# A range-test branch taken ahead of the last outputs, one output on another queue, and fewer closing waits

## The chip, the cores and the metric

The kernel runs on one core of one Trainium2 chip. The metric is the device time of one execution in microseconds (us), and of several executions the median. A profiled execution also has a *span*, from the first to the last instruction of the program; in most kernels here the time is 1.7 to 2.2 us longer than the span. The **tail** is the end of the span minus the end of the last matmul.

## The reference, cut to what matters

```python
# x: 2048 x 1024, 32 heads of 32
g = sigmoid((x * gate_w).sum(-1, keepdims=True))
a = linear_attention(x, A_wqkv) @ A_wo       # phi(t) = where(t > 0, t + 1, exp(t)) + 1e-6
b = local_attention(x, B_wqkv) @ B_wo        # 8 keys, every second position back; softmax
return g * a + (1 - g) * b
```

The kernel's fast path leaves out the subtraction of the row maximum in the softmax and folds some products. This is allowed only while the values lie in a certain range. It therefore computes maxima on the way, turns them into one flag, and at the end branches: if the flag is 0, a second complete program (the general path) computes everything again. With the given inputs the flag is 1, and the general path is jumped over.

## The kernel before

A small scheduler in Python places all operations of the fast path in time and emits them engine by engine; then each engine runs `tail`:

```python
def run(e, eng):                       # in Prog.emit
    for o, waits in plan[eng]:
        for s, v in waits:
            e.wait_ge(s, v)
        ins = o.fn(e)
        ins.then_inc(o.val[0], 16 if o.chan is not None else 1)
    tail(e, eng)

def tail(e, eng):
    reg = e.alloc_register("fast_ok")
    e.wait_ge(*flag_op.val)            # VectorE has written the flag
    e.reg_load(reg, flag[0:1, 0:1])
    if eng == "sp":
        for s, v in P.final:           # every DMA channel of the program: 80
            e.wait_ge(s, v)
    with e.If_eq(reg, 0):
        for s, v in P.final + [...]:   # (cut)
            e.wait_ge(s, v)
        for th in progs[eng]:          # the general path of this engine
            th(e)
```

The last stage computes 16 output tiles of 128 x 1024. For each half tile TensorE does 8 matmuls, VectorE combines the result with the other branch into the buffer `o` (two buffers in turn), and SyncE sends a whole tile to memory. The last tile goes in three pieces of 512, 256 and 256 columns:

```python
parts = [(0, 512), (512, 1024)] if t < NT - 1 else [(0, 512), (512, 768), (768, 1024)]
for f0, f1 in parts:
    # 8 matmuls into a bank of PSUM, then on VectorE the combine (cut)
    if t == NT - 1 or f1 == 1024:
        c = f0 if t == NT - 1 else 0
        P.op("sp", lambda e, ...: e.dma_start(out2[...], o_[:, c:f1]), 0.5, ..., chan="out%d_%d" % (os_, c))
```

Of the kernel before, what the change touches and what calls it, by code (L numbers as in the profile page):

```python
# [18 lines left out]
PADK = 16  # L19
PADV = 14  # L20
SCALE = DH ** -0.5
SZ = {BF16: 2, F32: 4, I32: 4}


class Tile:


    def __init__(self, space, h, lo, shape, dtype):
# [3 lines left out]
        for n in shape[1:]:  # L32
            self.row *= n
        self.size = SZ[dtype]

# [3 lines left out]
    def all(self):  # L39
        return [(self.space, self.lo, self.lo + self.row * self.size, self)]  # L40
# [21 lines left out]
class Prog:  # L62
# [136 lines left out]
                    ready(u, ready_at[u])  # L199
        self.span = max(free.values())  # L200

    def emit(self, block, tail):
        for e in self.ENGS:
            self.esem[e] = self.sem("e_" + e)
        chan_n = {}
        order = sorted(self.ops, key=lambda o: (o.start, o.seq))
        known_at = {}
        known = {e: {} for e in self.ENGS}
        plan = {e: [] for e in self.ENGS}
        cnt = {e: 0 for e in self.ENGS}  # L210
        for o in order:
            if o.chan is not None:
                if o.chan not in self.csem:
                    self.csem[o.chan] = self.sem("c_" + o.chan)
                chan_n[o.chan] = chan_n.get(o.chan, 0) + 16
                o.val = (self.csem[o.chan], chan_n[o.chan])
            else:
                cnt[o.eng] += 1
                o.val = (self.esem[o.eng], cnt[o.eng])
            need = {}  # L220
            k = known[o.eng]
            deps = sorted(o.deps, key=lambda d: -d.start)
            for d in deps:
                if d.eng == o.eng and d.chan is None:
                    if o.eng == "pe":
                        continue
                s, v = d.val
                if k.get(s.num, 0) >= v:
                    continue
                need[s.num] = (s, max(v, need.get(s.num, (s, 0))[1]))  # L230
                k[s.num] = max(k.get(s.num, 0), v)
                for s2, v2 in known_at[d].items():
                    if k.get(s2, 0) < v2:
                        k[s2] = v2
            known_at[o] = dict(k)
            plan[o.eng].append((o, list(need.values())))

        def run(e, eng):
            for o, waits in plan[eng]:
                for s, v in waits:  # L240
                    e.wait_ge(s, v)
                ins = o.fn(e)
                ins.then_inc(o.val[0], 16 if o.chan is not None else 1)
            tail(e, eng)

        self.final = [(self.csem[c], n) for c, n in chan_n.items()]
        self.counts = cnt
        block.sync(lambda e: run(e, "sp"))
        block.scalar(lambda e: run(e, "act"))
        block.tensor(lambda e: run(e, "pe"))  # L250
        block.vector(lambda e: run(e, "dve"))
        block.gpsimd(lambda e: run(e, "pool"))
# [63 lines left out]
def general_path(nc, A_x, A_wqkv, A_wo, B_wqkv, B_wo, gate_w, out):  # L316
# [254 lines left out]
    with ExitStack() as esA2:  # L571
# [40 lines left out]
        for jj, (kind, j) in enumerate(chunks):  # L612
# [13 lines left out]
            for u in range(NU):  # L626
# [28 lines left out]
                elif kind == "qB":  # L655
                    cA_q = pb.op("act", lambda e, j=j, ps_set=ps_set, scol=scol: e.activation(qT_sb[:, j, scol], ps_set, ACT.Copy, scale=SCALE),
                                 waits=[(sT, cT)], inc=sA)
# [445 lines left out]
def build_kernel(nc, A_x, A_wqkv, A_wo, B_x, B_wqkv, B_wo, gate_w, out):  # L1103
# [5 lines left out]
    out2 = out[0].rearrange("(m e) d -> e m d", e=2)  # L1109
# [4 lines left out]
    def SB(shape, dtype, name, at=None):  # L1114
        n = SZ[dtype]
        for d in shape[1:]:
            n *= d
        if at is None:
            at = base[0]
            base[0] += (n + 31) // 32 * 32  # L1120
        uid[0] += 1
        h = nc.alloc_sbuf_tensor_at("%s_%d" % (name, uid[0]), list(shape), dtype, offset=at)
        return Tile("S", h, at, list(shape), dtype)
# [94 lines left out]
    act = lambda n: 0.19 + n / 1200.0  # L1218
    dps = lambda n: 0.14 + n / 960.0

    def plan(seen):

        P = Prog(nc, nc.alloc_semaphore)
# [85 lines left out]
        def group(bank, lhs, rhs, reads, lo=0, hi=8):  # L1309
            def fn(e):  # L1310
                last = None
                for dc in range(lo, hi):
                    last = e.matmul(bank.ap(), lhs(dc), rhs(dc), start=(dc == 0), stop=(dc == 7))  # L1313
                return last
            return P.op("pe", fn, (hi - lo) * mm(512), reads=reads, writes=[bank.iv])
# [25 lines left out]
        def move(dst, src, n, bank, reg, scale=None, reads=()):  # L1341

            if scale is None:
                fd = lambda e: e.tensor_copy(dst, src())  # L1344
                fa = lambda e: e.activation(dst, src(), ACT.Copy)  # L1345
            else:
                fd = lambda e: e.tensor_scalar(dst, src(), scale, None, op0=ALU.mult)
                fa = lambda e: e.activation(dst, src(), ACT.Copy, scale=scale)  # L1348
            P.op("any", {"act": fa, "dve": fd}, {"act": act(n) + (0.1 if reads else 0.0), "dve": dps(n)}, reads=[bank.iv] + list(reads), writes=[reg])
# [7 lines left out]
        for t, half in [(4 * b + i, half) for b in range(NT // 4) for half in range(2) for i in range(4)]:  # L1357
# [5 lines left out]
            for d in range(0, 8, step):  # L1363
                o = group(bank, xs, w, [xr, ws[0].part((d, d + step), (half * 512, half * 512 + 512))], d, d + step)
# [87 lines left out]
        def slot(rate):  # L1452
            slot_n[0] += 1
            while later and later[0][0] <= slot_n[0]:
                later.pop(0)[1]()
            while states and states[0][0] <= slot_n[0]:
                states.pop(0)[1]()
            pace[0] = min(pace[0] + rate, 1.0) if todo else 0.0
            if todo and pace[0] >= 1.0:
                pace[0] -= 1.0  # L1460
                fill(*todo.pop(0))
# [6 lines left out]
        for e_ in range(2):  # L1468
            if True:
                for j in range(8):  # L1470
                    for isq in range(2):
                        for u in (2 * e_, 2 * e_ + 1):
# [6 lines left out]
                            reg = tgt.part((j, j + 1), (u * 512, (u + 1) * 512))  # L1479
                            move(dst, bank.ap, 512, bank, reg, SCALE if isq else None)  # L1480
                            slot(FILL)
# [63 lines left out]
        for c in range(4):  # L1545
            for r in range(4):
                k = 4 * (c % 2) + r
# [75 lines left out]
        def final(t):  # L1623
            tgt, c0 = a_loc(t)
            o_, os_ = osb.next()
            e_, r = t // 8, t % 8
            parts = [(0, 512), (512, 1024)] if t < NT - 1 else [(0, 512), (512, 768), (768, 1024)]
            for f0, f1 in parts:
                bank = main.next()
                n = f1 - f0  # L1630

                def fn(e, t=t, bank=bank, f0=f0, f1=f1):
                    for dc in range(8):
                        last = e.matmul(bank.ap(0, f1 - f0), qT[:, dc, t * 128:(t + 1) * 128], ws[3][:, dc, f0:f1], start=(dc == 0), stop=(dc == 7))  # L1634
                    return last
                P.op("pe", fn, 8 * mm(n), reads=[qT.part((0, 8), (t * 128, (t + 1) * 128)), ws[3].part((0, 8), (f0, f1))], writes=[bank.iv])
                i0, i1 = f0 // 128, f1 // 128
                P.op("dve", lambda e, bank=bank, o_=o_, t=t, n=n, i0=i0, i1=i1, tgt=tgt, c0=c0: e.scalar_tensor_tensor(  # L1638
                    out=o_[:, i0 * 128:i1 * 128].rearrange("p (i s) -> p i s", s=128), in0=bank.ap(0, n).rearrange("p (i s) -> p i s", s=128),
                    scalar=gm[:, t:t + 1], in1=tgt[:, i0:i1, c0:c0 + 128], op0=ALU.mult, op1=ALU.add), dps(n),  # L1640
                    reads=[bank.iv, gm.all(), tgt.part((i0, i1), (c0, c0 + 128))], writes=[o_.part((f0, f1))])
                if t == NT - 1 or f1 == 1024:
                    c = f0 if t == NT - 1 else 0
                    P.op("sp", lambda e, e_=e_, r=r, o_=o_, c=c, f1=f1: e.dma_start(out2[e_, r * 128:(r + 1) * 128, c:f1], o_[:, c:f1]), 0.5,
                         reads=[o_.part((c, f1))], chan="out%d_%d" % (os_, c), lat=1.0)

        nums = [(u, j) for u in range(4) for j in range(8)]
# [37 lines left out]
        flag_op = P.op("dve", lambda e: e.tensor_tensor(flag[:, :], mx1[:, 0:1], mx1[:, 2:3], ALU.mult), 0.1, reads=small, writes=[flag.all()], prio=1e5)  # L1685


        for t in range(EARLY, NT):
            final(t)
# [13 lines left out]
    P, flag_op = best[:2]  # L1703
    ps_guard.__exit__(None, None, None)
    progs, es_g = general_path(nc, A_x, A_wqkv, A_wo, B_wqkv, B_wo, gate_w, out)

    def tail(e, eng):
        reg = e.alloc_register("fast_ok")
        e.wait_ge(*flag_op.val)
        e.reg_load(reg, flag[0:1, 0:1])  # L1710
        if eng == "sp":
            for s, v in P.final:
                e.wait_ge(s, v)
        with e.If_eq(reg, 0):
            for s, v in P.final + [(P.esem[x], n) for x, n in P.counts.items() if n]:
                e.wait_ge(s, v)
            for th in progs[eng]:
                th(e)

    with nc.Block() as block:  # L1720
        P.emit(block, tail)
    es_g.__exit__(None, None, None)
    return P

# [31 lines left out]
```

## Time and profile before

| | before |
|---|---|
| time, median of 3 | 495.43 us (495.07 to 496.56) |
| span of the profiled execution | 493.6 us |
| TensorE busy | 477.7 us, 97% |
| end of the last matmul | 488.03 us |
| end of the last combine on VectorE | 488.55 us |
| tail | 5.61 us |

The page of the profiled execution shows what bounds the kernel (busy time, share, instructions, then the waits' chain by engine):

```profile
PE 477.7 (97%) x5055; PEld 226.2 (46%) x5121; DVE 274.7 (56%) x487; ACT 166.9 (34%) x287; POOL 5.1 (1%) x27
...
PE 89%; DMA 3%; SPq 3%; issue 2%; DVE 2%; ACT 1%; ACTq 0%
```

TensorE works nearly without a gap until 488. The timeline of the end (start, duration, engine, line, what) shows that nothing counted as work comes after 488.55, 5 us before the end:

```profile
485.37 4.03 SPq L1644 DMA_DIRECT2D out_dram<-o  x4
486.32 1.36 DVE L1638 SCALAR_TENSOR_TENSOR o<-ps_all,gm,xT 128x512 bf16<-128x512 f32 x2 [0.98 <-PE ps_all L1634]
488.07 0.48 DVE L1638 SCALAR_TENSOR_TENSOR o<-ps_all,gm,xT 128x256 bf16<-128x256 f32 x1 [0.39 <-PE ps_all L1634]
```

What happens in those 5 us is done by the engines' sequencers, and is seen when one asks for the lines of `tail` themselves. The columns are: how many, shortest/median/longest duration in ns, first and last start in us. Line 1710 is the load of the flag, 1713 the list of waits, 1714 the branch, 1720 the close of the program. The profile writes an engine's sequencer with a final q.

```profile
L1710 SPq TENSOR_LOAD <-flag x1: 503/503/503, 489.5 to 489.5; - x1
```

```profile
L1713 SPq EVENT_SEMAPHORE  x40: 28/28/28, 490.0 to 492.8; - x40
```

```profile
L1714 ACTq COMPARE_BRANCH  x1: 50/50/50, 443.7 to 443.7; - x1
L1714 PEldq COMPARE_BRANCH  x1: 3644/3644/3644, 486.3 to 486.3; - x1
L1714 DVEq COMPARE_BRANCH  x1: 72/72/72, 488.7 to 488.7; - x1
L1714 SPq COMPARE_BRANCH  x1: 58/58/58, 492.9 to 492.9; - x1
```

```profile
L1720 ACTq DRAIN  x1: 66/66/66, 446.1 to 446.1; - x1
L1720 PEldq DRAIN  x1: 73/73/73, 490.0 to 490.0; - x1
L1720 DVEq DRAIN  x1: 58/58/58, 491.5 to 491.5; - x1
L1720 SPq DRAIN  x1: 57/57/57, 493.4 to 493.4; - x1
```

Read the branch and the drain of an engine together. VectorE branches at 488.7 and does its next instruction at 491.5: the branch record says 72 ns, but the engine stood for 2.9 us. TensorE's sequencer stood for 3.6 us (its matmuls ran on meanwhile, until 488.03), ScalarE (443.7 to 446.1) for 2.4. In each of these stalls the trace shows a packet of instructions arrive: 8 KB from 489.70 to 490.16 in VectorE's, 8 KB from 444.57 to 445.00 in ScalarE's, 16 KB from 487.45 to 488.55 in TensorE's. I call such an arrival a fetch, and what one packet brings a block. (The packets come in two queues: 42 of 16 KB in one and, inside the span, 8 KB each in the other. I put the 16 KB queue down to TensorE and the other to the remaining engines, by the stalls that their packets fall into.) SyncE is the exception: 0.5 us from branch to drain.

### The profile page before, as it was taken

The page shows a single profiled execution, that of the slowest core. Times are in us where ns is not written, and L with a number is a line of the kernel's source. Part 1 is how long each engine was busy: PE and PEld are TensorE (multiplying, and loading weights), DVE is VectorE, ACT ScalarE, POOL GpSimd, SP SyncE. Part 2 cuts the span into 40 slices and gives each one's busy share as a digit, 9 for nine tenths or more (in the row PEclk, how much of TensorE's full clock was granted, in tenths as well). Part 3 has the DMA queues.
Part 4 walks back from the last instruction along what each step waited for, and adds up shares of the span by engine and source line. Part 5 has one row for each costly group of instructions (what it writes and reads, how often), then busy time and mean ns, then how long its engine had stood idle before and what let it go on. Part 6 is the DMA issues. An engine that isn't in the chain of part 4 may idle for free.

```text
span 493.6 us, 11394 instructions
## 1 busy us (share of the span) xinstructions
PE 477.7 (97%) x5055; PEld 226.2 (46%) x5121; DVE 274.7 (56%) x487; ACT 166.9 (34%) x287; POOL 5.1 (1%) x27
## 2 busy tenths in 40 slices
PE   8999999999999999999999999999999999999995
PEld 3444444444444445545554544444444444444442
DVE  2112345899676785564555555596865735524443
ACT  2111111222334345656565465455432223020000
POOL 3000000000000000000000000000000000000000
PEclk9999999999999999999999999999999999999999
DMA  8989992222003155111010100503564325101122
GB/s 225 212 206 322 307 371 62 86 86 85 14 23 110 29 161 141 28 36 35 24 35 25 35 3 3 171 1 80 124 182 117 76 38 153 65 1 66 65 85 68
DMA packets 51067, 48.80 MB, mean 99 GB/s; under 512 B 20161, under 2 KB 38977, under 8 KB 51010
## 3 DMA queue, kind: packets, MB, share of 16 engines
q1 hardware_dynamic: 50466, 47.47, 34.5%
q8 instruction: 42, 0.69, 0.6%
q10 hardware_dynamic: 544, 0.52, 0.3%
q14 instruction: 15, 0.12, 0.1%
HBM read 34.34 MB, written 9.44 MB: 89 GB/s over the span
## 4 chain that ended last, share of the span: by engine, by line
PE 89%; DMA 3%; SPq 3%; issue 2%; DVE 2%; ACT 1%; ACTq 0%
PE ps_all L1313 71%; PE ps_all L1634 11%; PE ps_all L1405 2%; PE ps_all L1424 2%; DMA rb<-rc_hbm 1%; SPq L1287 1%; PE ps_all L1506 1%; SPq L1598 1%; DMA w<-in_B_wqkv_dram 1%; PE ps_all L1431 1%; DMA rc_hbm<-ra 1%; DVE zsel L1548 1%; SPq L1292 1%; DVE pq L1326 0%; PE ps_all L1585 0%
## 5 line engine op out<-in xcount | busy, mean ns | idle before, releaser
L1313 PE MATMUL ps_all<-w,xT 128*128 128x512 bf16 x921 | 207.5, 380 | 5.4 <-issue 4.3
L1313 PE MATMUL ps_all<-xT,w 128*128 128x512 bf16 x748 | 167.5, 379 | 2.3 <-issue 1.7
L1313 PEld LDWEIGHTS ps_all<-w,xT 128*128 128x128 bf16 x960 | 91.3, 98 | 109.8 <-DMA xT<-in_A_x_dram 1.8
L1313 PEld LDWEIGHTS ps_all<-xT,w 128*128 128x128 bf16 x768 | 73.7, 98 | 89.1 <-issue 1.8
L1634 PE MATMUL ps_all<-w,qT 128*128 128x512 bf16 (+1 forms) x259 | 55.3, 373 | 0.3
L1634 PEld LDWEIGHTS ps_all<-w,qT 128*128 128x128 bf16 x264 | 25.8, 98 | 29.7
L1324 DVE TENSOR_SCALAR e<-e 128x512 bf16<-128x512 bf16 x64 | 18.3, 291 | 33.8 <-ACT e L1320 17.2
L1344 DVE CAST vst<-ps_all 128x512 bf16<-128x512 f32 x15 | 10.4, 692 | 44.0 <-PE ps_all L1313 44.0
L1411 ACT ACTIVATE E<-ps_all 128x1824 bf16<-128x1824 f32 (+1 forms) x18 | 30.4, 1687 | 9.8 <-PE ps_all L1405 9.0
L1322 ACT ACTIVATE e<-ps_all 128x512 bf16<-128x512 f32 x32 | 19.1, 597 | 42.8 <-PE ps_all L1313 42.8
L1414 DVE TENSOR_TENSOR E<-E,msk 128x1824 bf16<-128x1824 bf16 (+1 forms) x18 | 19.8, 1102 | 22.1 <-ACT E L1411 22.1
L1638 DVE SCALAR_TENSOR_TENSOR o<-ps_all,gm,xT 128x512 bf16<-128x512 f32 (+1 forms) x25 | 18.2, 730 | 23.0 <-PE ps_all L1634 22.8
L1320 ACT ACTIVATE e<-ps_all 128x512 bf16<-128x512 f32 x32 | 19.1, 597 | 26.8 <-PE ps_all L1313 25.8
L1345 ACT ACTIVATE vst<-ps_all 128x512 bf16<-128x512 f32 x17 | 10.1, 597 | 47.7 <-PE ps_all L1313 47.7
L1274 DVE TENSOR_TENSOR mx<-mx,kT 128x1024 bf16<-128x1024 bf16 x32 | 20.8, 688 | 9.3 <-ACT kT L1345 9.2
L1274 DVE TENSOR_TENSOR mx<-mx,qT 128x1024 bf16<-128x1024 bf16 x32 | 20.8, 687 | 6.9 <-ACT qT L1348 6.7
L1443 DVE TENSOR_TENSOR qT<-ps_all,L 128x456 bf16<-128x456 f32 (+1 forms) x36 | 21.0, 627 | 6.2 <-ACT L L1441 5.0
L1326 DVE SCALAR_TENSOR_TENSOR pk<-ps_all,e 128x512 bf16<-128x512 f32 x32 | 21.9, 688 | 0.7
L1440 ACT ACTIVATE L<-ps_all 128x456 f32<-128x456 f32 (+1 forms) x36 | 17.8, 547 | 12.4 <-PE ps_all L1424 12.4
L1345 ACT ACTIVATE kT<-ps_all 128x512 bf16<-128x512 f32 x16 | 9.6, 597 | 35.8 <-PE ps_all L1313 35.8
L1601 DVE TENSOR_TENSOR xT<-xT,rb 128x512 bf16<-128x512 bf16 x24 | 16.3, 689 | 8.7 <-DMA rb<-rc_hbm 8.5
L1348 ACT ACTIVATE qT<-ps_all 128x512 bf16<-128x512 f32 x16 | 9.6, 597 | 31.5 <-PE ps_all L1313 31.5
(72 smaller groups left out, 284.1 us busy)
## 6 DMA issues: line engine op xcount, KB each, us to landing
rb<-rc_hbm SPq DMA_DIRECT2D x32, 256.0 KB, 5.1
w<-in_A_wqkv_dram SPq DMA_DIRECT2D x6, 1024.0 KB, 8.5
v<-vB_hbm SPq DMA_DIRECT2D x36, 128.0 KB, 2.9
vB_hbm<-vst SPq DMA_DIRECT2D x32, 128.0 KB, 5.9
w<-in_B_wqkv_dram SPq DMA_DIRECT2D x4, 1024.0 KB, 9.0
xn<-in_A_x_dram SPq DMA_DIRECT2D x16, 256.0 KB, 2.7
out_dram<-o SPq DMA_DIRECT2D x15, 256.0 KB, 2.0
w<-in_A_wo_dram SPq DMA_DIRECT2D x8, 256.0 KB, 4.1
```

What stands on the lines that cost most here:

```text
L1274: P.op("dve", lambda e, m=m, op=op: e.tensor_tensor(m[:, 0:n], m[:, 0:n], src, op), 0.08 + n / 1920.0, reads=[m.all(), reg], writes=[m.all()],
L1313: last = e.matmul(bank.ap(), lhs(dc), rhs(dc), start=(dc == 0), stop=(dc == 7))
L1320: P.op("act", lambda e: e.activation(e_[:, :], bank.ap(), ACT.Exp), act(512), reads=[bank.iv], writes=[e_.all()])
L1322: P.op("act", lambda e: e.activation(e_[:, :], bank.ap(), ACT.Exp, accum_out=qe[:, col:col + 1]), act(512) + 0.1, reads=[bank.iv], writes= ...
L1324: P.op("dve", lambda e: e.tensor_scalar(e_[:, :], e_[:, :], 1.0, 1e-6, op0=ALU.min, op1=ALU.add), 0.25, reads=[e_.all()], writes=[e_.all()])
L1326: P.op("dve", lambda e: e.scalar_tensor_tensor(out=dst, in0=bank.ap(), scalar=0.0, in1=e_[:, :], op0=ALU.max, op1=ALU.add), dps(512), read ...
L1345: fa = lambda e: e.activation(dst, src(), ACT.Copy)
L1411: P.op("act", lambda e: e.activation(E[:, 0:32 * nq].rearrange("p (j q) -> p j q", j=4), ps[:, 4:8, 0:8 * nq], ACT.Exp), act(32 * nq), rea ...
L1414: P.op("dve", lambda e: e.tensor_tensor(ev(), ev(), m[:, :, :].rearrange("p r q -> p (r q)")[:, None, :].to_broadcast([128, 16, 2 * nq]), ...
L1443: P.op("dve", lambda e, L=L, h=h, q0=q0: e.tensor_tensor(qT[:, :, q0:q0 + nq], SO[h].ap(0, n).rearrange("p (c q) -> p c q", c=8), L[:, 0:n ...
L1634: last = e.matmul(bank.ap(0, f1 - f0), qT[:, dc, t * 128:(t + 1) * 128], ws[3][:, dc, f0:f1], start=(dc == 0), stop=(dc == 7))
L1638: P.op("dve", lambda e, bank=bank, o_=o_, t=t, n=n, i0=i0, i1=i1, tgt=tgt, c0=c0: e.scalar_tensor_tensor(out=o_[:, i0 * 128:i1 * 128].rear ...
```

## The change

The intent has three parts. (1) SyncE, VectorE and ScalarE take the branch *before* their last operations, and the remaining operations stand in both arms; the branch's stall then falls into time in which these engines have slack (19, 14 and 30 us ahead of the scheduled end; TensorE keeps its branch last). (2) The very last output piece is issued by ScalarE, not SyncE. (3) In the taken arm SyncE waits only for the four channels whose last transfer nobody has waited for.

```diff
+BACK = {"sp": 19, "dve": 14, "act": 30}
@@ emit
         def run(e, eng):
-            for o, waits in plan[eng]:
-                ...
-            tail(e, eng)
+            ops = plan[eng]
+            k = len(ops)
+            while k and ops[k - 1][0].start > max(self.span - BACK.get(eng, 0), flag_op.end + 3):
+                k -= 1
+            go(e, ops[:k])
+            tail(e, eng, lambda: go(e, ops[k:]))
+        self.last = [(self.csem[c], n) for c, n in chan_n.items() if not self.awaited(c)]
@@ final(t)
-                    P.op("sp", lambda e, ...
+                    P.op("act" if f1 == 1024 and c else "sp", lambda e, ...
@@ tail
-        if eng == "sp":
-            for s, v in P.final:
-                e.wait_ge(s, v)
         with e.If_eq(reg, 0):
+            rest()
             ...                        # (cut) waits and general path
+        with e.Else():
+            rest()
+            if eng == "sp":
+                for s, v in P.last:
+                    e.wait_ge(s, v)
```

## The prediction

> **What bounds the kernel.** TensorE. The page's busy table has PE at 477.7 of 493.6 us (97%), the granted clock at 0.998, and the chain of waits is 89% PE. The change touches none of this: no matmul, eviction or load goes away. It can only change what follows the last matmul.
>
> **The tail now** (timeline and raw instruction records of the last 8 us). The last matmul ends at 488.04, the last VectorE combine runs 488.07 to 488.55. SyncE issues the output in three last pieces: at 487.10 (0.33 us), 487.71 (1.22 us, unusually long) and 488.97 (0.43 us). So the last issue waits 0.42 us for the queue, not for its data. Then SyncE loads the flag (489.46, 0.50 us), executes 40 double semaphore waits from 490.00 to 492.82 (about 61 ns each after the first few, one pause of 0.4), branches at 492.86, drains at 493.36; the closing barrier ends at 493.64. The last output piece has landed by 490.68 (15 of 16 signals) or 491.05 (the last). So the wait list, not the transfer, ends last: about 1.8 us of it runs with nothing outstanding. The other engines' taken branches cost a fetch: GpSimd 2.5 us, ScalarE 2.4, VectorE 488.66 to 491.54 (2.9), TensorE 486.26 to 489.90 (3.6). [...] SyncE's own branch took only 0.5 us.
>
> **What the change does.**
> 1. Only four output channels remain to be waited for, instead of 80 semaphores: removes nearly all of the 2.8 us wait list. What then ends last is the landing.
> 2. Flag load, and branch of SyncE, move about 19 us ahead: takes 0.55 us between last issue and first wait and the 0.45 us closing jump off the end.
> 3. The last piece goes through ScalarE's idle queue: issue near 488.6 instead of 488.97; saves 0.3 to 0.4 us of landing. The middle piece on SyncE (landed 490.04 to 490.28) then ends about as late.
> 4. VectorE's load and fetch (0.54 + 2.9 us) move to about 475. This stalls VectorE in the output stage, where it has 0.75 us of work per 1.73 us of TensorE: the next combine is about 2.5 us late, and 0.98 us is recovered per combine, so it is level by 482. Spare PSUM banks keep TensorE going. SyncE's fetch falls after the issue at 468.1, with 3.4 us to the next: at most one output a little late. TensorE's branch stays where it is, ending at 489.96, just ahead of the new end.
>
> New end, estimated: last landing 490.3 to 490.6, last waits 0.1, drain 0.06, barrier 0.28: 490.7 to 491.1. So 2.5 to 2.9 us come off the span, all on the critical path (0.5%); the rest of the changed work was hidden before and stays hidden.
>
> **Prediction: 492.7 us, range 491.9 to 493.5 (8 in 10). Faster by over 2%: 0.01; within 2%: 0.98; slower by over 2%: 0.01.**
>
> **What would show it.** Span near 490.9; last combine still ending near 488.55; no SyncE list of waits after the last issue; the end within 0.6 us of the last landing; PE gapless through 470 to 488; VectorE with one hole of about 3.5 us near 475 and shorter gaps after it until about 482; last issue on ScalarE's queue near 488.6.
>
> **What would make it wrong.** The hole in VectorE or SyncE reaching TensorE through PSUM or the two output buffers (then over 494); another fetch stall at the end of the taken arm (up to 3 us given back); TensorE's fetch getting longer and setting the end; the last piece's issue on ScalarE being as slow as SyncE's 1.22 us, or its landing held by a fetch; another operation order chosen by the scheduler.

## The result and the profile after

| | before | after |
|---|---|---|
| time, median of 6 | 495.5 us (495.07 to 496.56) | 492.72 us (491.94 to 494.49) |
| ratio | 1 | 0.9949 (0.9927 to 0.997) |
| span of the profiled execution | 493.6 us | 492.6 us |
| end of the last matmul in it | 488.03 us | 489.52 us |
| tail | 5.61 us | 3.10 us |

Ratios in this document are the mean time of one kernel's fast runs over the mean of the other's fast runs of the same rounds, so they are not quite the ratio of the medians.

The profiled execution of after happens to be its slowest (494.49 us; the spans of the other five are 490.1 to 492.4). Its first matmul after the warm-up began at 6.47 us instead of 5.62, and its last ended 1.5 us later than in the profile of before. Of these 1.5 us, 0.85 are the start; the rest arises on the way, and the other five spans show that it is not typical. It is why the two profiled spans differ by only 1.0 us while the tails differ by 2.5.

The lines of `tail` after (1724 is the branch, 1734 the waits, 1736 the close):

```profile
L1724 ACTq COMPARE_BRANCH  x1: 50/50/50, 445.1 to 445.1; - x1
L1724 SPq COMPARE_BRANCH  x1: 57/57/57, 470.5 to 470.5; - x1
L1724 DVEq COMPARE_BRANCH  x1: 72/72/72, 476.3 to 476.3; - x1
L1724 PEldq COMPARE_BRANCH  x1: 3704/3704/3704, 487.8 to 487.8; - x1
```

```profile
L1734 SPq EVENT_SEMAPHORE  x2: 17/22/28, 492.1 to 492.1; - x2
```

```profile
L1736 DVEq DRAIN  x1: 524/524/524, 489.6 to 489.6; - x1
L1736 ACTq DRAIN  x1: 152/152/152, 490.5 to 490.5; - x1
L1736 PEldq DRAIN  x1: 73/73/73, 491.5 to 491.5; - x1
L1736 SPq DRAIN  x1: 13/13/13, 492.4 to 492.4; - x1
```

SyncE now ends when the last output has landed, 2.54 us after the last matmul. All branches over the general path but TensorE's are over long before. (SyncE has one more branch, at the end of its arm: its record says 43 ns, and the next instruction begins 0.17 us after it.) So the sum was forecast well. But two things in the profile do not fit the forecast. The first is VectorE's hole, in the timeline of VectorE:

```profile
475.73 0.75 DVE L1651 SCALAR_TENSOR_TENSOR o<-ps_all,gm,xT 128x512 bf16<-128x512 f32 x1 [0.97 <-PE ps_all L1647]
482.20 2.73 DVE L1651 SCALAR_TENSOR_TENSOR o<-ps_all,gm,xT 128x512 bf16<-128x512 f32 x4 [5.72 <-issue]
485.77 1.41 DVE L1651 SCALAR_TENSOR_TENSOR o<-ps_all,gm,xT 128x512 bf16<-128x512 f32 x2 [0.85 <-DMA out_dram<-o]
487.81 1.36 DVE L1651 SCALAR_TENSOR_TENSOR o<-ps_all,gm,xT 128x512 bf16<-128x512 f32 x2 [0.63 <-PE ps_all L1647]
```

It is 5.72 us, not 3.5, and VectorE is level with TensorE again only at 487.2, 2.3 us before the last matmul ends; on the way it waits 0.85 us for an output buffer to be sent (third line). The second is that one output issue of SyncE took 1.28 us, as one had before (1.22 us), with a queue that had little to do (columns as above):

```profile
L1644 SPq DMA_DIRECT2D out_dram<-o x4: 332/382/1222, 485.4 to 489.0; - x4
```

```profile
L1657 SPq DMA_DIRECT2D out_dram<-o x3: 332/332/1278, 487.2 to 489.2; - x3
L1657 ACTq DMA_DIRECT2D out_dram<-o x1: 365/365/365, 490.1 to 490.1; - x1
```

### The profile page after: what moved, and what is told of

It is laid out like the page before. It is cut to its first block, busy times and chain, and to the rows that moved or that the text cites. A ratio compares the mean times of both kernels' runs of the same rounds, so it can differ in the third digit from the quotient of the medians.

```text
span 492.6 us, 11357 instructions
## 1 busy us (share of the span) xinstructions
PE 478.7 (97%) x5055; PEld 226.9 (46%) x5121; DVE 274.4 (56%) x487; ACT 166.9 (34%) x287; POOL 5.0 (1%) x27
## 4 chain that ended last, share of the span: by engine, by line
PE 91%; DMA 3%; DVE 2%; issue 2%; SPq 1%; ACT 1%; ACTq 0%
PE ps_all L1326 74%; PE ps_all L1647 11%; PE ps_all L1418 2%; PE ps_all L1437 2%; DMA rb<-rc_hbm 1%; DMA xT<-in_A_x_dram 1%; PE ps_all L1519 1%; SPq L1611 1%; PE ps_all L1444 1%; DMA rc_hbm<-ra 1%; DVE zsel L1561 1%; DVE pq L1339 0%; PE ps_all L1598 0%; PE ps_all L1571 0%; DVE e L1337 0%
```

## The experiments

A table first. Kernels are compared only within the same rounds.

| run | what | tail, us | time, us | ratio to before |
|---|---|---|---|---|
| before | | 5.61 | 495.5 | 1 |
| after | the change | 3.10 | 492.72 | 0.9949 |
| e1 | before, short waits only | 5.97 | 496.0 | 1.0012 |
| e2 | change, with all waits | 3.91 | 493.24 | 0.9955 |
| e3 | change, one queue | 3.12 | 492.52 | 0.9942 |
| e4 | change, branch late | 5.18 | 495.19 | 1.0004 |
| e5 | e1, the dropped waits placed early | 4.04 | 495.59 | 1.0003 |
| e6 | change, VectorE's arm moved by 8 | 2.99 | 492.35 | 0.9939 |
| e7 | change, VectorE 8 us ahead, not 14 | 5.94 | 496.39 | 1.0016 |
| e8 | e7 and e6 together | 3.12 | 492.33 | 0.9945 |
| e9 | e5, VectorE's landing moved by 8 | 3.92 | 493.32 | 0.9956 |
| e10 | change, TensorE's branch later | 5.26 | 494.3 (one run) | not timed |
| e11 | e6, prefetch hint for TensorE | 2.99 | 492.40 | 0.9933 |
| e12 | e4, hints for four engines | 4.63 | 494.24 | 0.9973 |

All twelve gave the right result. Each tail is read from one profile. The five kernels after, e3, e6, e8 and e11, in which the last outputs set the end and not a branch, have tails of 2.99 to 3.12 us, so I read nothing from a difference of about 0.1 us.

### What each part is worth

**e1: only the short waits, in the kernel before.**

```diff
         if eng == "sp":
-            for s, v in P.final:
+            for s, v in P.last:
```

> The kernel before, with only its long list of closing waits cut to the four output channels; branch still last, all outputs on SyncE. I read the tail: end of the span minus the end of the last matmul (before 5.60 us, after 3.10). My theory: the list was the end of the critical path, but behind it VectorE's late taken branch (drain at 491.54 in the profile of before) and SyncE's own load, landing and jump are nearly as long. So the tail becomes 3.7 to 3.9 us, about 1.8 us faster than before[...]. Rival: the list is the whole gain; then the tail is that of the change, 3.1.

Measured: tail 5.97 us, 0.36 us *longer* than before, and the time did not fall (ratio 1.0012, interval 0.9996 to 1.0028). Both theories fell. The output landed as before and two waits replaced forty, but look at SyncE's branch and drain:

```profile
L1715 SPq COMPARE_BRANCH  x1: 58/58/58, 491.2 to 491.2; - x1
```

```profile
L1721 DVEq DRAIN  x1: 57/57/57, 491.6 to 491.6; - x1
L1721 SPq DRAIN  x1: 57/57/57, 493.8 to 493.8; - x1
```

SyncE's branch now stalls for 2.57 us, where it took 0.5 before. The list of waits had paid for the branch. What made the difference is the subject of e5.

**e2: the change with the full list of waits.**

```diff
         with e.Else():
             rest()
             if eng == "sp":
-                for s, v in P.last:
+                for s, v in P.final:
```

> The change with the full list of waits put back on SyncE in the taken arm. My theory: SyncE's last issue ends 0.96 us after the last matmul; then some 40 waits at 61 ns, 2.5 to 2.85 us, and 0.45 us to close: tail 4.0 to 4.3 us, about 1.1 us slower than the change. Rival: the list only fills time in which the output lands; then the tail stays at 3.1.

Measured: tail 3.91 us, time 493.24 us. The 40 double waits run from 1.05 to 3.46 us after the last matmul, about 60 ns each. So, behind an early branch, the short list is worth 0.8 us of the tail (the times, 493.24 and 492.72 us, do not separate the two kernels). My theory's number was 0.1 us too high; its rival is refuted.

**e3: the change with one queue.**

```diff
-P.op("act" if f1 == 1024 and c else "sp", ...
+P.op("sp", ...
```

> The change with the last output issued by SyncE again. My theory: the last issue waits for the slow issue before it (1.28 us), so it starts 0.4 us later than on ScalarE and the tail is 3.3 to 3.6 us instead of 3.1. Rival: the second last piece, which stays on SyncE in both, lands last anyway; then the tail stays within 0.1 us of 3.1.

Measured: tail 3.12 us against 3.10, time 492.52 us. My theory fell, the rival holds. ScalarE does issue the last piece 0.39 us sooner (0.56 us after the last matmul instead of 0.95), but the middle piece then lands later. With two queues the middle piece has landed at 2.54 us and the last at 2.38; with one queue they landed at 2.16 and 2.62. The later of the two is what counts, and it moved by 0.08 us. Against e6 and e11, which also have two queues (tails of 2.99 us), the gap is 0.13 us, so these tails leave at most that for the second queue. In this pair of runs the second queue saved issue time, not landing time; why the middle piece lands later is not shown.

**e4: the change with the branch last.**

```diff
-BACK = {"sp": 19, "dve": 14, "act": 30}
+BACK = {}
```

> The change with all work before the branch (no head start for any engine), short waits and two queues kept. My theory: VectorE now starts load and branch after its last combine: 0.5 + 0.6 + 2.9 to 3.3 us of fetch + 0.3: tail 4.3 to 4.7 us. [...] Rival: the branch costs nothing here because the landing of the output covers it; then 3.1 to 3.3.

Measured: tail 5.18 us, time 495.19 us, the time of before. My range was 0.5 us too low, because the slowest branches were not VectorE's:

```profile
L1724 DVEq COMPARE_BRANCH  x1: 72/72/72, 488.1 to 488.1; - x1
L1724 ACTq COMPARE_BRANCH  x1: 54/54/54, 488.9 to 488.9; - x1
L1724 SPq COMPARE_BRANCH  x1: 58/58/58, 489.1 to 489.1; - x1
```

```profile
L1736 DVEq DRAIN  x1: 58/58/58, 490.9 to 490.9; - x1
L1736 ACTq DRAIN  x1: 61/61/61, 492.3 to 492.3; - x1
L1736 SPq DRAIN  x1: 12/12/12, 492.4 to 492.4; - x1
```

Three branches at nearly the same moment stall for 2.9 us (VectorE), 3.4 (ScalarE, which now branches after the last issue) and 3.0 (SyncE, from the branch to its first wait). The head start of the branch is therefore worth 5.18 - 3.10 = 2.1 us of the 2.5, beside the two other parts. How it divides among the three engines was not tested; in e4 SyncE and ScalarE come last, and VectorE 1.4 us before them.

### Why the long list had made SyncE's branch cheap

**e5: e1 with the dropped waits walked through early.**

```diff
             for o, waits in plan[eng]:
+                if not told and o.start > self.span - 12:   # SyncE, ahead of its last few outputs
+                    told = True
+                    for s, v in self.final:
+                        if (s, v) not in self.last:
+                            e.wait_ge(s, v)
```

> The kernel before with short closing waits (as in e1_waits_only, where the tail was 5.97 us because SyncE's closing branch took 2.57 us instead of 0.5), but the other 38 double waits are not dropped: they stand ahead of SyncE's last few outputs, where the queue is idle and all of them are long met. My theory: [...] With the list walked through early, the branch again takes about 0.5 us: tail 3.8 to 4.0 us (landing 3.04, waits 0.1, branch 0.5, barrier 0.3). Rival: the branch was quick in the kernel before because SyncE was late and something else had been done by then (time, not place); then it again takes 2.6 us and the tail stays near 6.0.

Measured inside the span: tail 4.04 us, and 0.50 us from SyncE's branch to its drain.

```profile
L1721 SPq COMPARE_BRANCH  x1: 58/58/58, 492.0 to 492.0; - x1
```

```profile
L1727 DVEq DRAIN  x1: 58/58/58, 492.2 to 492.2; - x1
L1727 SPq DRAIN  x1: 57/57/57, 492.5 to 492.5; - x1
```

SyncE reaches the branch at nearly the same time after the last matmul as in e1 (3.26 us; 3.12 there) with the same two waits ahead of it. Only the *place* of the branch in the instruction stream differs, by about 40 instructions. The rival, that being late made it quick, is refuted. The traces show the place itself. In before and in e5 the list of waits pauses once, for 0.40 us, each time behind the same (207th) instruction of SyncE's stream, and 0.63 us after the pause an 8 KB instruction packet follows: 1.3 us ahead of the branch in before, 13.9 us ahead in e5. In e1 SyncE branches at its 201st instruction, short of that place, and the packet comes only 0.9 us *after* the branch. So the branch took 0.50 us where SyncE had passed that place before it, and 2.57 us where it had not. The list of waits in the kernel before was not pure waste; it walked SyncE forward to where its jump was short (0.5 us).

But the *time* did not fall: 495.59 us, ratio 1.0003. The saved 1.57 us must reappear outside the span. Time minus span shows it: 3.2 to 3.5 us in all six runs of e5, 1.8 to 2.2 in those of before, and 2.2 to 2.4 in e4, the only other kernel above the rest.

**e9: e5 with VectorE's landing point moved by eight instructions.** The padding is sixteen waits that are long met, at the end of VectorE's general path, which never runs; they compile to eight instructions. The same edit makes e6 from the change.

```diff
             for th in progs[eng]:
                 th(e)
+            if eng == "dve":
+                for _ in range(16):
+                    e.wait_ge(*flag_op.val)
```

> The kernel of e5_waits_early with eight instructions added at the end of VectorE's general path. In e5 the tail inside the span fell to 4.04 us (before 5.61) but the time did not fall: time minus span was 3.2 to 3.5 us, where all kernels but one have 1.7 to 2.0. My theory: [...] the next block, which holds what runs after the last profiled instruction, comes about 2.1 us after VectorE's drain; in the kernel before the span ends 2.1 us after that drain, so it was hidden, in e5 only 0.6 us after. With the landing point moved eight on, time minus span is 1.7 to 2.0 again and the time 1.3 to 1.7 us below before. Rival: the extra belongs to SyncE or to the early waits; then time minus span stays at 3.2 to 3.5 and the time is that of before.

Measured: time minus span 1.7 to 1.9 us again, time 493.32 us, ratio 0.9956 (0.9942 to 0.997), 2.2 us below before. This was more than the 1.3 to 1.7 expected; the tail itself also came out 0.12 us shorter than in e5, which is within the spread of tails. So the hidden cost was VectorE's: only the place where its jump lands was changed. My account of it, which the records do not show directly, is that the jump landed next to the edge of a block, and that the next block was still on its way when the profiled program ended. VectorE drains 2.1 us before the end of the span in before (no extra), 1.7 in e4 (extra of about 0.4), 0.6 in e5 (extra of about 1.4): each pair adds up to 2.0 or 2.1 us. The instructions after the span are not in the records, so that they are what waits is inferred from these sums and from e9. The instruction packets fit: e5's trace ends with one at 6.53 us after the last matmul, 2.5 us after the end of the span, and e9's has none after 4.79 us; whose packet it is, the trace does not say.

### VectorE's hole

**e6: the change with the same padding.**

> The change with eight instructions added for VectorE at the end of the arm that never runs, so that VectorE's taken arm starts eight instructions later. In the change VectorE's hole was 5.72 us (476.48 to 482.20), with a first stall of 3.3 us after the branch, one instruction, and a second stall of 2.6. My theory: the arm's first instruction is the last of a block, and the second stall is the fetch of the next block; with the arm moved eight on, the hole is 3.0 to 3.4 us. Rival: the second stall is a wait (for an output buffer or TensorE) or belongs to the branch itself; then the hole stays at 5.7. Both expect the time of the change within 0.3 us, since VectorE is level again before the end.

Measured: the hole, timeline of VectorE:

```profile
474.44 0.75 DVE L1651 SCALAR_TENSOR_TENSOR o<-ps_all,gm,xT 128x512 bf16<-128x512 f32 x1 [0.97 <-PE ps_all L1647]
477.95 1.41 DVE L1651 SCALAR_TENSOR_TENSOR o<-ps_all,gm,xT 128x512 bf16<-128x512 f32 x2 [2.77 <-PE ps_all L1647]
```

2.77 us instead of 5.72, from eight instructions that are never executed. It repeats: in the five profiles with the unmoved arm (after, e2, e3, e7, e10) the hole is 5.04 to 5.72 us, in the three with the moved one (e6, e8, e11) 2.77 each time. The hole of the change was two stalls: 3.3 us from the branch to the first instruction of the arm, then 2.6 us from that instruction to the next, which I read as the step into the next block; an 8 KB instruction packet falls into each (11.7 and 9.1 us before the end of the last matmul). The estimate of 3.0 to 3.4 was a little high. The time is that of the change (492.35 us; 0.9939, interval 0.9924 to 0.9953).

**e7 and e8: VectorE's head start 8 us instead of 14, without and with the padding.**

```diff
-BACK = {"sp": 19, "dve": 14, "act": 30}
+BACK = {"sp": 19, "dve": 8, "act": 30}
```

> The change with VectorE's head start cut from 14 to 8 us (five combines after the branch instead of nine). My theory: the hole of 5.7 us starts at about 7.2 us before the last matmul's end; five combines are then done back to back from about 1.5 us before the last matmul's end, and the last one ends 1.6 to 2.0 us later than it would: tail 4.7 to 5.1 us instead of 3.1. Rival: VectorE's idle time in this stage (0.98 us of each 1.73) absorbs it; tail 3.1 to 3.3.

> As e7_back8, with the eight instructions added to VectorE's arm that never runs. My theory: the hole is 3.0 to 3.4 us, two or three combines are late, the last three are on time: tail 3.1 to 3.2 us, the time of the change, 1.6 to 2.0 us below e7_back8. Rival (the place of the arm does not matter): the same tail as e7_back8.

Measured, e7:

```profile
482.97 0.75 DVE L1651 SCALAR_TENSOR_TENSOR o<-ps_all,gm,xT 128x512 bf16<-128x512 f32 x1 [0.97 <-PE ps_all L1647]
489.08 2.85 DVE L1651 SCALAR_TENSOR_TENSOR o<-ps_all,gm,xT 128x512 bf16<-128x512 f32 x5 [5.36 <-PE ps_all L1647]
```

and e8:

```profile
480.78 0.75 DVE L1651 SCALAR_TENSOR_TENSOR o<-ps_all,gm,xT 128x512 bf16<-128x512 f32 x1 [0.98 <-PE ps_all L1647]
484.30 1.41 DVE L1651 SCALAR_TENSOR_TENSOR o<-ps_all,gm,xT 128x512 bf16<-128x512 f32 x2 [2.77 <-PE ps_all L1647]
```

In e7 the five remaining combines are done back to back after the hole, and the last ends 2.07 us after the last matmul instead of 0.52: 1.55 us late. The tail is 5.94 us, 2.8 longer than the change's, so the late combines cost more than the 1.6 to 2.0 expected; the last output also landed late, 3.3 us after ScalarE began to issue it (1.8 in the change), which I did not test: fifteen of that piece's sixteen signals are in at 3.72 us after the last matmul and the last comes at 5.44, and a 16 KB packet of TensorE's instructions runs from 2.83 to 4.22. The time is 496.39 us, slightly *slower* than before (1.0016, interval 1.0004 to 1.0028). In e8 the hole is 2.77 us, the combines are level again, the tail is 3.12 us and the time 492.33. The change's 14 us were enough, but with 2.3 us to spare; at 8 us the whole gain hangs on where the arm happens to start.

### SyncE's slow issue

In nine of the ten profiles taken before this run (before, after, e1 to e8), a 16 KB instruction fetch of TensorE (a packet of the 16 KB queue) began 0.76 to 0.34 us before the end of the last matmul and ended 0.44 to 0.62 us after it. In eight of these SyncE began an output issue at -0.32 us, inside the fetch, and it took 1.22 to 1.32 us. In the ninth, e7, nothing was issued then. In the tenth, e8, where this fetch began at 0.04 us, the issue took 0.33:

```profile
L1657 SPq DMA_DIRECT2D out_dram<-o x3: 332/332/333, 485.7 to 487.3; - x3
```

**e10: TensorE waits for VectorE's last combine before it loads the flag** (slower on purpose).

```diff
         reg = e.alloc_register("fast_ok")
+        if eng == "pe":
+            e.wait_ge(P.esem["dve"], P.counts["dve"])
```

> The change with TensorE made to wait for VectorE's last combine before it loads the flag and branches; deliberately slower, to move TensorE's 16 KB instruction fetch away from the output issues. In nine of ten profiles that fetch ran from about -0.6 to 0.6 us (from the last matmul's end) and SyncE's second last issue, begun at -0.32, took 1.22 to 1.32 us; in the one where the fetch came at 0.04 it took 0.33. My theory: the fetch holds the issue. With the fetch moved to after 1.5 us the issue takes 0.33 us, and the tail grows to 4.7 to 5.2 us by TensorE's branch. Rival: the queue is slow at its third issue in a short time; then it still takes 1.2 to 1.3 us.

Measured, the output issues of the end:

```profile
L1657 SPq DMA_DIRECT2D out_dram<-o x2: 332/332/333, 486.3 to 486.9; - x2
L1657 ACTq DMA_DIRECT2D out_dram<-o x1: 365/365/365, 487.8 to 487.8; - x1
```

The fetch has moved to 2.12 us and the issue takes 0.33 us, three issues in close order or not. All outputs have landed at 2.17 us instead of 2.54. The tail is 5.26 us, just above my range, because TensorE's branch comes last. So it is the fetch of one engine that held the output issue of another. The ends agree with that: in all eleven profiles with a slow issue (those eight, e9, e11 and e12) the issue ends 0.38 to 0.39 us after the packet does; in e12, where the packet ends earliest (0.34 us), the issue takes 1.05 us. By what path is not shown.

The fetch goes with late transfers too. In the twelve profiles in which the piece issued at -0.93 us met this fetch, its last signal came at 1.52 to 2.30 us; in e10 it came at 0.78, and fifteen of the sixteen were in by 0.78 in all thirteen.

**e11: e6 with a prefetch hint for TensorE's branch.** The branch is written out with its two targets in the same order of code, and an instruction that names it is placed about 8 us ahead.

```diff
+                if o.eng in HINT and o.eng not in hints and o.start > self.span - HINT[o.eng]:
+                    hints[o.eng] = e.mark_branch_hint_location()
...
+            e.br_ne(reg, 0, on_true=fin, on_false=gen).branch_hint(hint)
```

> The kernel of e6_pad with a prefetch hint for TensorE's closing branch placed about 8 us before its end, and that branch written out with the same order of code. My theory: the target is then fetched early, the branch takes under 0.6 us instead of 3.6 to 3.7, no 16 KB fetch meets the output pieces, SyncE's second last issue takes 0.33 us, no output signal comes late: tail 2.6 to 2.8 us against 2.99 to 3.1. Rival: [...] the branch takes 3.6 us and the tail stays at 3.0 to 3.1.

Measured, TensorE's branch (line 1731) and the output issues (line 1662):

```profile
L1731 PEldq COMPARE_BRANCH  x1: 401/401/401, 486.5 to 486.5; - x1
```

```profile
L1662 SPq DMA_DIRECT2D out_dram<-o x3: 333/333/1362, 485.6 to 488.0; - x3
```

The branch fell from 3.6 to 0.4 us, as my theory said, and the fetch ran 8.1 us before the end of the last matmul. But the tail stayed at 2.99 us, as the rival said, though with a short branch: the next packet of TensorE's queue ran from -0.62 to 0.65 us, and the same issue was held again (1.36 us). That packet began about 0.8 us after the end of the branch's record, as in before and after (0.78 us in both), so I take it that it came early because the branch was over early. The ratio, 0.9933 (0.9919 to 0.9948), does not separate this kernel from the change or from e6.

**e12: all work before the branch, with hints on four engines instead of two arms.** The code is that of e4 with the written-out branch of e11 on every engine but GpSimd.

> The kernel of e4_late_branch (all work before the branch, tail 5.18 us) with such hints on SyncE, ScalarE, VectorE and TensorE, each ahead of the last outputs; no work is doubled into two arms. My theory: the head start of the change is worth its time only because it hides the fetch, so hints do the same: tail 2.7 to 3.4 us, the time of the change within 0.5 us. Rival: the flag load and branch themselves, or a hint that does not take, keep it at 4.5 to 5.2.

Measured: tail 4.63 us, time 494.24 us. My theory fell; the rival, that a hint does not take, holds. Only TensorE's hint took (0.40 us). On the other three the branch stalled as ever: from branch to drain VectorE stood for 3.0 us, ScalarE for 2.6, and SyncE for 2.7 to its first wait, though the trace has all four hint instructions as executed. Between 45 us before the last matmul's end and 1.8 us after it, the only instruction packets in the trace are those of TensorE's queue, so the three other hints started no fetch that it shows. Why is open. The doubled arms are still the fastest here, but they are not the only way: e9, with the branch last, one queue and no doubled work, has a ratio of 0.9956 (0.9942 to 0.997), which these runs do not separate from the change's 0.9949 (0.9927 to 0.997).

## Why the prediction was right or wrong, point by point

- **The time.** 492.7 us was forecast and 492.72 measured; 2.5 to 2.9 us off the span were forecast, and the tail fell by 2.51. The agreement to 0.02 us is luck, for the six runs spread over 2.6 us. That TensorE's work before the tail would not move was right (busy for 16.45 of the 16.5 us up to 489.5).
- **"What then ends last is the landing."** Right: SyncE's last wait is met within 0.1 us of the last landing, which came 2.54 us after the last matmul (forecast 2.3 to 2.6), and the span ends 0.56 us after it (forecast 0.44). The forecast end was made by following this path, not by adding up the parts, and that is why it held. "Just ahead of the new end" for TensorE was right too (drain at 491.5, end at 492.6).
- **"Only four output channels remain to be waited for ... removes nearly all of the 2.8 us wait list."** As one of three terms to be added up, this was wrong. Alone the short list gained nothing (e1, tail +0.36 us); behind an early branch it gained 0.8 (e2). The step that failed is the observation that "SyncE's own branch took only 0.5 us", which I took as a property of the branch. It was a property of its place, and the list supplied that place (e5). The parts do not add; the whole came out because all of them were done together.
- **The branch ahead of time.** I counted 0.55 and 0.45 us for SyncE. Beside the other two parts its worth was 2.1 us (e4), since it hides three stalls at once (2.9, 3.4 and 3.0 us in e4), one of which the shorter list makes longer (SyncE's: 0.5 us in before, 2.57 in e1).
- **"Saves 0.3 to 0.4 us of landing" by ScalarE's queue.** Wrong: 0.02 us (e3), 0.13 at most. The issue moved as forecast, by 0.39 us; the landing did not, because the middle piece got later. That the landing still came as early as forecast was in part luck: it was at 3.02 us in before and at 2.62 with one queue (e3), because the last piece's sixteenth signal came 0.37 us after the fifteenth in before and 0.02 in e3. Why was not tested.
- **VectorE "about 2.5 us late ... level by 482".** The mechanism was right, the size was not: the hole was 5.72 us and VectorE was level 2.3 us before the last matmul's end, not 6. The missing term is a second stall of 2.6 us, which was gone when the arm was moved by eight instructions (e6). It remained hidden with 2.3 us to spare. The risk that I named as "the hole in VectorE or SyncE" is real at a shorter head start (e7).
- **SyncE's fetch "at most one output a little late".** Right: the output after its branch began 0.13 us after its data was ready.
- **"1.22 us, unusually long".** Noted and left unexplained; it was TensorE's fetch (e10).

## What to carry to other kernels

Here a jump over a large piece of code cost 2.4 to 3.7 us (before: ScalarE 2.4, GpSimd 2.5, VectorE 2.9, TensorE 3.6; e4: SyncE 3.0, ScalarE 3.4, TensorE 3.7), except on SyncE behind the list of waits (0.5 us, before and e5) and on TensorE with a hint (0.40 us, e11 and e12). The branch's own record shows it only on TensorE; on the others that record is 45 to 84 ns, and the stall lies between it and the next instruction. Take such a jump where that engine has slack, and check the size of the hole and the time at which the engine is level again. The stall depended on where the branch (SyncE, 0.50 us in e5 and 2.57 in e1) and its target (VectorE's hole, 2.77 us in e6 and 5.72 in after) lay in the instruction stream, so instructions that never run, or waits that are long met, can change the time: when an edit at the end gives nothing, compare each engine's branch and the next instruction after it before concluding that the removed work was free. Read parts of a change together, because a part that is worthless alone can be worth 0.8 us beside another, and compare the time with the span, since a cost can slip out of the profiled part (time minus span was 3.2 to 3.5 us in e5, 1.7 to 1.9 in e9). A fetch of one engine held the DMA issue of another here: SyncE's 0.33 us became 1.05 to 1.36 while TensorE fetched 16 KB.
